# Softmax weights scaled where the output is written, the logarithm ahead of the dummy products, and a new instruction order, in a fused recurrence and soft-expert kernel

## The chip, the core and the metric

The kernel runs on one core of a Trainium2 chip. The metric is the device time of one execution in microseconds (us). The kernel before takes 120.81 us (median of three runs, 120.77 to 120.97). The core's engines run side by side, each with its own queue of instructions in program order: TensorE (PE; its weight loads are listed as PEld), VectorE (DVE), ScalarE (ACT), GpSimd (POOL) and SyncE (SP). An engine whose next instruction waits lets everything behind it wait as well.

## What is computed

There are two stages, one feeding the other.

```
# stage 1, for each of 4 batches x 8 heads, head width 48, 768 steps
cur   = (u * k_t) outer v_t
y_t   = r_t @ (state + cur)
state = w * state + k_t outer v_t
# stage 2, x is y as 3072 tokens x 384; 8 experts with 4 slots each
logits = x @ phi                       # 3072 x 32
d = softmax of logits over the tokens (each column)
slot_input = d.T @ x                   # 32 x 384
slot_out = relu(slot_input @ w1[e]) @ w2[e]      # for each expert e
c = softmax of logits over the slots (each row)
out = c @ slot_out                     # 3072 x 384, float32
```

The first softmax is called dispatch here, the second one combine.

## The kernel before, in words

**Stage 1.** The 768 steps are cut into six chunks `c` of 128 steps. In each chunk, k, r and v arrive by two transfers each (`iL0` to `iL35`, two for each k, r, v of a chunk, in that order). They are copied into a padded tile (`qk`, `qr`, `qv`, line 325), transposed by TensorE (`tk`, `tr`, `tv`, line 335) and evicted, with k and r multiplied by tables of powers of w (`ek`, `er`, line 345) and v plain (`ev`). Transposing back gives natural-layout copies (`bk`, `bv`, line 356; evictions `kn`, `vn`). For each of two batch pairs `bl` and two head halves, TensorE forms the scores (`A`, line 374), VectorE masks them (`M`, line 380, 24 of them), TensorE adds up the outputs (`Y`, lines 448 to 456), and `x` evicts them. The state products are `s` (lines 420 and 424), their evictions with decay `S` (line 432). The diagonal term with `u` needs `pr` (line 386, k times r, on VectorE or GpSimd), a small product `D` (line 396), its eviction `ds` and `dv` (line 403, v times `ds`), which `Y` adds.

**Stage 2** starts chunk by chunk. `X` transposes x, `xT` evicts it, `l` forms the logits and `lg` evicts them. The combine softmax of a chunk (function `slots`, lines 493 to 523) goes: `mx` row maxima (VectorE), `sb` subtraction (GpSimd or VectorE), `ex` exponential (ScalarE), `sr` row sums and reciprocals (VectorE), `cn` division with a fourfold copy (GpSimd or VectorE), `c` transposes (TensorE), `cT` eviction. The dispatch softmax runs over three groups of chunks: maxima `gm`, `gt`, `gr`, their exchange over partitions `gd`, `gb`, `gx`; `gs` subtraction, `ge` exponential, `dp` products, `acc` running sums, with the rescaling `gf`, `gg`, `am` between groups. The last group takes its maxima from logits formed a second time (`gl`, line 558).

**The last chain.** After the last `acc`, `rc` and `un` divide by the column sums; `h00` to `h11` (line 662) multiply by w1, `hs` applies the maximum with 0, `ht` transposes, `hT` evicts, `o00` to `o77` (line 689) multiply by w2 and `so` evicts the result. Then 24 products `p` (line 713), their evictions `oe` (line 716, ScalarE and VectorE in turn) and eight transfers write the output.

**Transfers.** GpSimd issues all loads of k, r, v (`iL`), w1 (`iW0` to `iW7`) and w2 (`iV0` to `iV6`, `iVa7` for seven eighths and `iVb7` for the last eighth of the last expert) on one queue. From the ninth on, each issue first waits until the load eight places before it has landed (line 271). w2 lands in the space that raw k, r, v held. Output transfers are issued by SyncE.

**The order** is written out by hand: `ORDER` lists all steps, and `Plan.emit` issues them as listed, so each engine's queue is that list cut down to its own steps. A token such as `qr0:1/D` means step `qr0`, buffer 1, engine D (DVE), A (ACT) or P (POOL). Dummy products (`fill`, line 220, 128x512 each) run at the start: three, then four ahead of the logarithm on line 259, which the tables of powers (`zt`, `ze`) need.

Of the kernel before, what the change touches and what calls it, by code (L numbers as in the profile page):

```python
# [12 lines left out]
ORDER = """
zb zc iL4 za zd:/A zt1 iL5 zt2 ze1 iL6 qk0:0/D ze2 iL7 zt3 tk00:0,0 iL8 zt0 ze3 iL9 tk01:1 ze0 iL10 qr0:1/D ek00
iL11 tr00:2,0 ek01 tr01:3 iL12 er00 qv0:0/A iL13 bk00:4,0 er01 bk01:5,1 iL14 pr0:0/D kn00:/A A000:0,0 tv00:0,0
qk1:1/A iL15 tv01:1 kn01:/D D0:2,0 M000 iL16 ev01:/A tk10:3,1 tk11:4 iL17 ev00:/D qr1:0/A A001:0,1 ek10 bv00:5,0
iL18 bv01:1,1 ek11 ds0:/A vn00:/A tr10:0,1 M001 iL19 tr11:3 qv1:1/A dv00:0/P s00:2,4,0 bk10:5,2 er10 A010:0,2
vn01:/A S100 bk11:0,0 iL20 qk2:0/D tv10:2,1 kn10:/A dv01:1/P er11 Y001:1 kn11:/A S101 s01:5,3,1 pr1:0/D ev10:/A
tv11:4 iL21 Y000:0,0 iL22 ev11:/A S110 D1:2,1 iL23 x000:/D ds1:/A x001:/A S111 iL24 bv10:5,2 qr2:1/A M010 bv11:4,3
iL25 X00:0,0 iL26 xT00:/D vn10:/A Y010:2,1 iL27 vn11:/D A011:0,1 x010:/A l00:1 dv10:0/P s10:3,0,2 M011 lg00:/A  # L20
tk20:5,0 tk21:4 S200 iL28 tr20:2,0 ek20 iL29 qv2:0/A Y011:1 S201 A100:0,0 iL30 s11:3,5,3 er20 dv11:1/P x011:/A M100
tv20:0,0 tv21:2 ev20:/A X01:1,1 iL31 S210 A101:0,2 xT01:/D iL32 ev21:/A Y100:3,2 S211 iL33 tr21:0 qk3:0/D x100:/A
l01:1 iL34 bv20:5,0 M101 qr3:1/A bv21:2,1 iL35 vn21:/D Y101:3 vn20:/A iW0 er21 A110:0,1 lg01:/A x101:/A ek21 iW1
X10:2,0 M110 pr2:0/P bk20:5,1 xT10:/A bk21:1,2 mx0 kn20:/A A111:0,0 kn21:/D Y110:0,3 M111 tk30:3,1 x110:/A tk31:4
s20:2,1,0 ek30 qv3:0/A ek31 A200:0,2 Y111:5 S300 iW2 D2:0,0 S301 sb0:0/P tv30:3,1 x111:/A M200 iW3 s21:4,2,1 ds2:/A
ex0 ev30:/A dv20:0/P X11:1,1 tr30:5,1 sr0 xT11:/A A201:0,1 S310 tv31:0 iW4 S311 tr31:3 er30 dv21:1/P ev31:/A l11:4
Y200:1,4 M201 bk30:2,0 lg11:/A qk4:0/A iW5 bv30:5,2 x200:/D A210:0,0 cn0:0/P bv31:0,3 er31 vn30:/A bk31:4,1 M210
iW6 Y201:1 vn31:/A pr3:0/P c0:3 qr4:1/A l10:5 kn30:/D A211:0,2 Y210:0,5 lg10:/D x201:/D s30:2,5,2 M211 kn31:/A
X20:1,1 x210:/A tk40:4,0 S400 cT0:/A tk41:0 xT20:/D A300:0,1 ek40 qv4:0/A Y211:2 iW7 M300 D3:3,1 l20:1 zu tr40:4,0
x211:/A S401 ds3:/A lg20:/A A301:0,0 iV0 tr41:2 er40 dv30:0/P tv40:3,0 M301 qk5:1/A X21:1,0 tv41:5 xT21:/D iV1  # L30
A310:0,2 ev40:/A er41 dv31:1/P l21:4 ek41 ev41:/A s31:1,2,3 M310 bk40:3,2 iV2 lg21:/A qr5:0/A bk41:0,0 pr4:0/P
bv40:5,0 S410 bv41:4,1 gm0 kn41:/A Y301:1 S411 kn40:/A gt0:0 A311:0,0 mx2 gr00 Y300:2,6 vn41:/A mx1 M311 tk50:3,1
vn40:/A tk51:0 Y310:4,7 ek50 x300:/A iV3 qv5:1/A A400:0,1 ek51 Y311:5 sb1:1/P M400 iV4 D4:2,0 x301:/A s40:3,0,0
sb2:0/P x311:/A X30:1,1 gd0 ex2 x310:/D iV5 ex1 gb0:5 A401:0,2 ds4:/A sr2 xT30:/A s41:4,2,1 dv40:0/P gx0 M401
X31:5,0 l30:1 xT31:/A gs0:/P S510 A410:0,0 lg30:/D Y401:4 S501 dv41:1/P M410 ge0 tr50:1,1 tr51:5 l31:0 er50
A411:0,2 iV6 lg31:/A tv50:0,1 er51 tv51:1 M411 ev50:/A pr5:0/P dp0:5 ev51:/A mx3 sr1 Y411:0 acc0 cn1:1/D Y400:5,0
S500 bv50:1,2 x401:/A sb3:1/D A500:0,2 x400:/D vn50:/A bv51:3,3 M500 c1:4 ex3 Y410:5,1 iVa7 vn51:/A D5:1,1 cn2:0/P
sr3 x410:/A A501:0,1 X40:3,1 x411:/D ds5:/A cT1:/A M501 iVb7 X41:5,0 xT40:/A cn3:1/P c2:1 l40:0 dv50:0/D xT41:/A
A510:0,0 dv51:1/P c3:4 cT2:/A M510 l41:3 Y501:5 cT3:/A Y500:1,2 lg41:/A lg40:/A S511 A511:0,1 x500:/A Y510:4,3 gm1
x501:/A mx4 gt1:3 M511 sb4:0/P X50:0,1 x510:/A ex4 xT50:/A sr4 Y511:2 gr10 cn4:0/P gl0:1 gd1 x511:/D gb1:5 l50:4  # L40
gr20 X51:0,0 gx1 lg50:/A c4:3 gf1:/D gs1:/P xT51:/D gg1 cT4:/A am1:/D gl1 ge1 l51:2 dp1:5 gr21 lg51:/A gd2 mx5
gb2:4 sb5:1/D acc1 ex5 gs2 gx2 sr5 ge2 gf2:/P dp2:0 gg2 cn5:1/D am2:/P c5:3 acc2 rc cT5:/D un1:/P un0 h10:1 h01:2
hs10:/D h00:5 hs01:/D h11:4 hs00:/D ht0:0 hs11:/D hT0:/D ht1:3 o00:1 hT1:/D o10 o20 o30 o40 o50 o60 o70 o77 so p0:2
p1:5 oe0 p2:4 oe1 p3:0 dm00 oe2 p4:3 oe3 p5:1 dm01 oe4 p6:2 oe5 p7:5 dm02 oe6 p8:4 oe7 p9:0 oe8 p10:3 dm04 oe9
p11:1 p12:2 oe10 p13:5 oe11 p14:4 oe12 p15:0 p16:3 oe13 oe14 p17:1 dm10 p18:2 oe15 oe16 p19:5 p20:4 oe18 oe17 p21:3
dm14 p22:0 oe20 oe19 p23:2 oe22 oe21 dm20 oe23 dm24
# [712 lines left out]
```

## Time and profile before

| what | value |
|---|---|
| median of the runs | 120.81 us |
| the profiled execution, whole | 120.92 us |
| its span, first to last instruction | 119.1 us |
| busy: PE, DVE, ACT, POOL | 79%, 82%, 61%, 60% of the span |
| moved by DMA | 24.67 MB, mean 207 GB/s |
| bytes on the loads' queue | 19.66 MB |

The span is the stretch that the profile covers; 1.8 us of the execution lie outside it. Times in rows are microseconds from the start of the span. In the page's strips the span is cut into 40 slices of 2.98 us; a digit is the share in tenths, 9 for 90% and more. A row of the timeline gives start, length, engine, line, operation, tiles written and read, and in brackets how long the engine was idle before it and what released it. Rows of one line are merged, x24 being 24 instructions; the lengths of neighbouring rows overlap a little, because an instruction starts before the one ahead has drained. A row of windows gives for a stretch its length, the busy time of each engine, the granted TensorE clock as a share, the busy share of the DMA engines and the rate.

### The profile page before, as it was taken

Reading aid. Unit: us, or ns where it says so; the run is one execution under the profiler, and the core shown is the slowest. Engines: PE = TensorE matmul, PEld = TensorE weight load, DVE = VectorE, ACT = ScalarE, POOL = GpSimd, SP = SyncE. Lnnn points to the kernel's source line nnn. Section 1 sums busy time; section 2 is a strip of 40 time slices with the busy share of each in tenths; the row PEclk is TensorE's granted clock in tenths of the full one; section 3 lists DMA queues with packets and bytes.
Section 4 is the critical chain, followed back from the end, with each engine's and each line's share of the span. In section 5 each row is a group of like instructions: output and inputs, shape, how many; then the busy total and the mean of one; then the engine's idle time right before and its main releaser. Section 6 shows DMA issues by size and latency. Waiting matters only on the chain.

```text
span 119.1 us, 3755 instructions
## 1 busy us (share of the span) xinstructions
...
## 2 busy tenths in 40 slices
...
PEclk9999999999999999999999999999985559999855
DMA  2999999999999999999999999999999991049994
GB/s 28 155 171 199 207 207 207 212 192 193 210 203 207 229 213 219 210 217 216 217 210 221 210 221 214 213 215 218 215 215 219 206 189 25 0 175 417 411 415 167
DMA packets 8992, 24.67 MB, mean 207 GB/s; under 512 B 1168, under 2 KB 6160, under 8 KB 8976
## 3 DMA queue, kind: packets, MB, share of 16 engines
q0 software_dynamic: 7632, 19.66, 86.1%
...
q8 instruction: 12, 0.20, 0.6%
q14 instruction: 4, 0.03, 0.1%
q10 hardware_dynamic: 24, 0.00, 0.0%
...
## 4 chain that ended last, share of the span: by engine, by line
PE 34%; DVE 29%; DMA 10%; issue 7%; POOL 7%; ACT 4%; DVEq 0%; POOLq 0%; ACTq 0%
DMA w_all<-in_moe_w_dram 10%; PE pG L335 8%; DVE AT L380 8%; PE pG L662 4%; POOL pr L386 3%; PE pG L713 3%; DVE S L432 3%; PE pG L356 3%; DVE cn L510 2%; PE pG L689 2%; PE pA L374 2%; DVE rT L345 2%; DVE dv L403 2%; PE pA L222 2%; ACT rp L199 2%
## 5 line engine op out<-in xcount | busy, mean ns | idle before, releaser
L380 DVE TENSOR_TENSOR AT<-pA,mask 128x1024 bf16<-128x1024 f32 x24 | 29.1, 1214 | 0.2
L335 PE MATMUL pG<-ident,rp 128*128 128x128 bf16 x288 | 21.0, 230 | 3.0 <-DVE rp L201 3.0
L199 ACT COPY rp<-raw 128x1536 bf16<-128x1536 bf16 x14 | 20.8, 1486 | 3.5 <-PE pG L335 1.8
L335 PEld LDWEIGHTS <-rp 128*128 128x128 bf16 x288 | 18.2, 103 | 4.8 <-DVE rp L201 3.9
L403 POOL TENSOR_TENSOR dv<-vn,ds 128x768 bf16<-128x768 bf16 x11 | 16.3, 1480 | 3.2 <-ACT vn L199 2.0
L386 POOL TENSOR_TENSOR pr<-kT,rT 128x2048 bf16<-128x2048 bf16 x4 | 16.3, 4067 | 1.5 <-DVE rT L345 0.9
L199 ACT COPY w_all<-pG 128x384 f32<-128x384 f32 x12 | 4.9, 499 | 12.3 <-PE pG L713 12.3
L199 ACT COPY vT<-pG 128x1024 bf16<-128x1024 bf16 x11 | 10.8, 1025 | 1.8 <-PE pG L335 1.8
L432 DVE TENSOR_TENSOR S<-pG,W 128x384 bf16<-128x384 f32 x20 | 10.8, 546 | 0.0
L374 PE MATMUL pA<-rT,kT 64*128 64x128 bf16 x192 | 9.6, 218 | 0.4 <-DVE AT L380 0.3
L454 PE MATMUL pG<-vn,AT 128*128 128x48 bf16 x192 | 8.7, 183 | 1.2 <-DVE AT L380 1.2
L199 ACT CAST x<-pG 128x384 bf16<-128x384 f32 x17 | 8.2, 498 | 2.1 <-PE pG L456 2.1
L199 ACT COPY vn<-pG 128x768 bf16<-128x768 bf16 x10 | 7.9, 815 | 1.0 <-PE pG L356 1.0
L356 PE MATMUL pG<-ident,vT 128*128 128x128 bf16 x96 | 6.7, 219 | 1.9 <-DVE S L432 1.9
L211 POOL DMA_DIRECT2D raw<-in_k_dram x12 | 6.6, 564 | 2.6 <-DMA raw<-in_v_dram 1.8
L211 POOL DMA_DIRECT2D raw<-in_v_dram x12 | 6.8, 579 | 2.2 <-DMA raw<-in_r_dram 2.2
L345 DVE TENSOR_TENSOR kT<-pG,Tk 128x1024 bf16<-128x1024 bf16 x12 | 7.8, 681 | 0.3 <-ACT Tk L299 0.3
L454 PEld LDWEIGHTS <-AT 128*128 128x128 bf16 x192 | 7.0, 96 | 1.7 <-DVE AT L380 1.7
L345 DVE TENSOR_TENSOR rT<-pG,Tr 128x1024 bf16<-128x1024 bf16 x12 | 8.0, 680 | 0.0
L456 PE MATMUL pG<-dv,ident 128*128 128x384 bf16 x24 | 7.7, 323 | 0.3 <-DVE dv L403 0.3
L374 PEld LDWEIGHTS <-kT 64*128 64x128 bf16 x192 | 5.8, 94 | 2.8 <-issue 1.2
L211 POOL DMA_DIRECT2D raw<-in_r_dram x12 | 6.6, 562 | 1.0 <-DMA raw<-in_k_dram 0.9
(123 smaller groups left out, 213.9 us busy)
## 6 DMA issues: line engine op xcount, KB each, us to landing
w_all<-in_moe_w_dram POOLq DMA_DIRECT2D x8, 768.0 KB, 15.0
raw<-in_moe_w_dram POOLq DMA_DIRECT2D x7, 768.0 KB, 23.8
out_dram<-w_all SPq DMA_DIRECT2D x5, 768.0 KB, 4.8
raw<-in_k_dram POOLq DMA_DIRECT2D x12, 192.0 KB, 6.7
raw<-in_r_dram POOLq DMA_DIRECT2D x12, 192.0 KB, 6.5
raw<-in_v_dram POOLq DMA_DIRECT2D x12, 192.0 KB, 6.7
...
out_dram<-w_all SPq DMA_DIRECT2D x2, 192.0 KB, 2.0
```

What stands on the lines that cost most here:

```text
L199: O(act.copy(dst, src))
L211: O(pool.dma_start(out=raw_t(x)[:, bb * JJ * D:(bb + 1) * JJ * D], in_=src[c, bb]))
L335: O(pe.transpose(o[:, :, j, :], rp_r[W[rp]][:, jh * JH + j].rearrange("p b d -> p (b d)"), ident[:]))
L345: O(dve.tensor_mul(dst, src, (Tk, Tr)[which][:, None, jh].to_broadcast(BC)))
L356: O(pe.transpose(bank_b(kb)[:, h * C:(h + 1) * C], src[:, bl, h].rearrange("p a x -> p (a x)"), ident[:]))
L374: O(pe.matmul(pA[:, bb, h4 * C:(h4 + 1) * C], kt[s, bl, h].rearrange("p a x -> p (a x)"), rt[s, bl, h].rearrange("p a x -> p (a x)"), star ...
L380: O(dve.tensor_mul(AT_r[W[f"AT{key}"]][:], pA[:].rearrange("p bb (h t) -> p bb h t", t=C), mask[:, None, None, :].to_broadcast([128, 2, H ...
L386: O(op(e).tensor_mul(pr_r[W[f"pr{c}"]][:], kT_r[W[f"kT{c}"]][:].rearrange("p a h j x -> p a h (j x)"), rT_r[W[f"rT{c}"]][:].rearrange("p a ...
L403: O(op(e).tensor_mul(dv_r[W[f"dv{c}{bl}"]][:], vn_r[W[f"vn{c}{bl}"]][:], ds_r[W[f"ds{c}"]][:, bl, :, :, None].to_broadcast([128, H, 2, D])))
L432: O(dve.tensor_mul(S_r[W[new]][:, s], bank(kb[hf])[:, 0:HD].rearrange("p (h b d) -> p h b d", b=2, d=D), W128[:, s, :, None].to_broadcast( ...
L454: O(pe.matmul(o[:, z:z + D], AT_r[W[at]][:, bb, h4, :], vn[:, hf * H2 + h4, bb, :], start=(c == 0 and h4 == 0 and bb == 0), stop=False, sk ...
L456: O(pe.matmul(o[:, 0:HD], ident[:], dv_r[W[f"dv{c}{bl}"]][:, hf * H2:(hf + 1) * H2] .rearrange("p h b d -> p (h b d)"), start=False, stop= ...
```

## The change

1. **Combine softmax.** `sb`, `sr` and `cn` are gone. `mx` writes the negated maximum; `ex` is four ScalarE instructions for a chunk (one for each batch) that read the logits four times over, take the maximum as bias and write the unnormalised weights in bfloat16 straight to `cn`'s tile. The row sums come from TensorE: `rs`, 24 products with a column of 32 ones, and `rr`, one reciprocal. The evictions `oe` multiply by it.
2. **Start.** The logarithm stands ahead of the four dummy products. Two small memsets (line 248 and 249 of the new file) fill the column of ones.
3. **Dummy products** `F0` to `F24`, one 128x512 product each, stand between the steps of the last chain.
4. **Order.** The whole list is new. `dv` is on GpSimd always.

```diff
@@ slots
-        P.add(f"sb{c}", "POOL|DVE", lambda e: O(op(e).tensor_sub(
-            ee_r[W[f"ee{c}"]][:], lg, mx[:, c, :, None].to_broadcast([128, B, ES]))), deps=[f"mx{c}"],
-            take=[(f"ee{c}", "ee")])
         def ex(e):
-            t = ee_r[W[f"ee{c}"]]
-            O(act.activation(out=t[:], in_=t[:], func=AF.Exp))
+            for b in range(B):
+                O(act.activation(out=cn_r[W[f"cn{c}"]][:, b], in_=lg_all[:, c * B + b:c * B + b + 1, :]
+                                 .to_broadcast([128, 4, ES]), func=AF.Exp, bias=mx[:, c, b:b + 1]))
-            O(dve.tensor_reduce(out=sm[:, c], in_=ee_r[W[f"ee{c}"]][:], axis=AX.X, op=ALU.add))
-            O(dve.reciprocal(sm[:, c], sm[:, c]))
-        P.add(f"cn{c}", "POOL|DVE", lambda e: O(op(e).tensor_mul(
...
@@ new steps
+    def sums(e):
+        for i in range(3 * JH):
+            g, j = divmod(i, JH)
+            O(pe.matmul(bank("rsb")[:, i:i + 1], cT[:, j, g * 128:(g + 1) * 128], one_s[:], start=(i == 0), stop=True,
+                        skip_group_check=True))
+    P.add("rr", "DVE", lambda e: O(dve.reciprocal(rcs[:], bank("rsb")[:, 0:3 * JH])), deps=["rs"], use=["rsb"])
@@ eviction of the output
-                    e, obuf[:, i * Dm:(i + 1) * Dm], bank(kb)[:, 0:Dm]), deps=[f"p{i}"], use=[kb]))
+                    if e == "ACT":
+                        O(act.mul(dst, src, rcs[:, i:i + 1]))
+                    else:
+                        O(dve.tensor_scalar(out=dst, in0=src, scalar1=rcs[:, i:i + 1], scalar2=None, op0=ALU.mult))
@@ start
+    O(act.activation(out=lnw[:], in_=pA[:, 1, 0:H], func=AF.Ln))
     fill(4)
-    O(act.activation(out=lnw[:], in_=pA[:, 1, 0:H], func=AF.Ln))
@@ dummy products
+FILL = [("gt1", 3), ("gl0", 2), ("X51", 3), ("gl1", 3), ("dp1", 3), ("gb2", 4), ("dp2", 4), ("acc2", 3)]
+    for after, count in FILL:
+        for x in range(count):
+            P.add(f"F{n}", "PE", lambda e: fill(1), deps=[after, f"F{n - 1}" if n else None])
```

The new order, cut down to the queues that the prediction speaks of (a minus is before, a plus is after):

```diff
 VectorE, start
- zb za zt1 zt2 qk0 zt3 zt0 qr0 ek00 ek01 er00 er01
+ zt1 zt0 zt2 zt3 qk0 za zb qr0 ek00 ek01 er00 er01
 GpSimd
- iL19 dv00 iL20 dv01 iL21 iL22 iL23 iL24 iL25 iL26 iL27 dv10 iL28 ... iL35 iW0 iW1 pr2 iW2 sb0 iW3 dv20 iW4 dv21
+ iL19 dv00 iL20 dv01 iL21 iL22 pr1 iL23 iL24 iL25 iL26 iL27 iL28 dv10 iL29 dv11 iL30 ... iL35 dv20 iW0 iW1 iW2 iW3 dv21
- iW7 zu iV0 dv30 iV1 dv31 iV2 pr4 iV3
+ iW7 iV0 pr3 iV1 zu dv30 iV2 dv31 iV3 pr4 iV4 dv40 iV5 dv41 gs0 pr5 iV6 iVa7 dv50 iVb7 dv51
 VectorE, end
- M511 sr4 gr10 gd1 x511 gr20 gx1 gf1 xT51 am1 gr21 gd2 mx5 sb5 acc1 gs2 gx2 sr5 cn5 acc2 rc cT5 un0 hs10 hs01 hs00 hs11 hT0 hT1 so
+ M511 gm1 mx4 x511 gr10 gr20 gd1 xT51 gx1 gs1 gr21 gd2 mx5 acc1 gs2 gx2 gf2 cT5 acc2 rc un0 hs00 hs11 hs10 hT1 rr hs01 hT0 so
 ScalarE, end
- ex4 xT50 lg50 gg1 cT4 ge1 lg51 ex5 ge2 gg2
+ xT50 ex4 lg50 cT4 gg1 ge1 lg51 ex5 ge2 gg2
 TensorE, end
- gl0 gb1 l50 X51 c4 gl1 l51 dp1 gb2 dp2 c5 h10 h01 h00 h11 ht0 ht1 o00
+ gt1 F0 gl0 l50 X51 F1 c4 gb1 F2 gl1 l51 F3 F4 F5 F6 dp1 gb2 F7 c5 F8 F9 F10 dp2 F11 ... F17 h00 h11 h10 F18 ... F22 ht1 F23 rs F24 h01 ht0 o00
```

Across the whole list, VectorE loses six `sr`, two `cn`, two `sb`, one `dv`, one `am`, two `x` and one `xT`, and takes over from ScalarE or GpSimd two padded copies `q`, one `kn`, one `vn`, one `ev`, three `ds`, two `lg`, one `cT` and `gs1`. The numbers of masks, state evictions, `ek`, `er` and `pr` (two on VectorE, four on GpSimd) stay. `pr1` goes from VectorE to GpSimd, `pr2` the other way.

More of the change, by code (lines that the diff above doesn't have):

```diff
@@ L16 @@
[L16 to L20, printed above, removed]
@@ L31 @@
[L31 to L35, printed above, removed]
@@ L41 @@
[L41 to L45, printed above, removed]
```

79 lines of the change are left out of this document (48 added, 31 removed).

## The prediction

> **What bounds the kernel now.** I read the page's strips first, then a table of windows that cuts the span where the stages change, then the timeline at the seams.
>
> ```profile
> span 119.1 us, 3755 instructions
> ...
> PEclk9999999999999999999999999999985559999855
> DMA  2999999999999999999999999999999991049994
> ```
>
> ```profile
> 9.94:63.41 53.47, 51.03 (x954) 44.16 (x953) 52.20 (x82) 46.85 (x63) 46.37 (x54) 1.00 1.10 210
> 63.41:87.27 23.86, 19.78 (x386) 16.30 (x385) 23.38 (x40) 14.17 (x30) 15.26 (x14) 1.00 1.04 215
> 87.27:94.20 6.93, 4.83 (x81) 3.58 (x81) 5.43 (x21) 2.40 (x8) 2.04 (x4) 0.59 1.04 215
> 94.20:100.58 6.38, 6.13 (x64) 2.67 (x65) 3.37 (x6) 0.00 (x0) 0.00 (x0) 0.65 0.68 133
> 100.58:103.44 2.86, 2.78 (x65) 1.71 (x65) 0.69 (x1) 0.00 (x0) 0.00 (x0) 1.00 0.03 6
> 103.44:119.10 15.66, 4.89 (x24) 2.21 (x23) 6.22 (x13) 4.94 (x12) 0.00 (x0) 0.79 0.75 301
> ```
>
> Busy columns are PE, PEld, DVE, ACT, POOL, then granted clock, DMA share, GB/s. Up to 63.41 VectorE (52.20 of 53.47) and TensorE (51.03) are both full. From there to 87.27, where the last x is evicted, VectorE alone is full and TensorE is idle for 23.86 - 19.78 = 4.1 us. Then a chain of small steps runs at a falling clock, the w1 products at about half clock, the w2 products, and 15.66 us of output, which is a matter of transfers (301 GB/s on average) and which I hold fixed. Independently of all this, the DMA strip is at 9 from 3 us to about 98 us: the loads are a second bound. Where do they end?
>
> ```profile
> 76.04 0.59 POOL L217 DMA_DIRECT2D raw<-in_moe_w_dram  x1
> ```
> ```profile
> raw<-in_moe_w_dram POOLq DMA_DIRECT2D x1, 96.0 KB, 24.1
> ```
>
> The last eighth of w2 is issued at 76.04 and lands 24.1 us later, at 100.15. o77 needs it, and `so` needs o77. Now `so` starts at 103.44, so **whatever the engines gain, 3.2 us is the most that can be won** unless the loads end earlier, and every delay of the loads eats into that.
>
> **Start.** Terms 1 to 4 give when the w2 products can be done, term 5 when the loads let them.
>
> ```profile
> 5.89 0.18 ACT L259 ACTIVATE lnw<-pA 128x8 f32<-128x8 f32 x1 [3.25 <-PE pA L222]
> ...
> 9.44 0.51 POOL L211 DMA_DIRECT2D raw<-in_v_dram  x1 [0.49 <-DMA raw<-in_r_dram]
> ...
> 9.94 0.55 DVE L201 COPY rp<-raw 128x1536 bf16<-128x1536 bf16 x1
> ```
>
> (1) The logarithm loses its wait on the dummy products (3.25 us idle). What is late next is data: qr0, the copy at 9.94, needs the second r transfer, whose landing releases GpSimd at 9.44. In the new VectorE queue qr0 stands ahead of ek00, so VectorE stands there till 9.44. Gain 9.94 - 9.44 = 0.5 us, not 3. The two memsets and zd, za, zb fit in that wait.
>
> **The body.**
>
> ```profile
> L510 DVE TENSOR_TENSOR cn<-ee,sm 128x512 bf16<-128x512 f32 x2 | 3.6, 1815 | 0.0
> ...
> L403 DVE TENSOR_TENSOR dv<-vn,ds 128x768 bf16<-128x768 bf16 x1 | 2.0, 1974 | 0.0
> L201 DVE COPY kn<-pG 128x768 bf16<-128x768 bf16 x3 | 1.7, 551 | 0.0
> ...
> L507 DVE TENSOR_REDUCE sm<-ee 128x4 f32<-128x128 f32 x6 | 1.6, 274 | 0.0
> ...
> L497 DVE TENSOR_TENSOR ee<-lg_all,mx 128x128 f32<-128x128 f32 x2 | 1.1, 563 | 0.1
> ...
> L508 DVE RECIPROCAL sm<-sm 128x4 f32<-128x4 f32 x6 | 1.1, 178 | 0.2
> ```
>
> (2) VectorE loses 3.6 (cn) + 2.0 (dv) + 1.6 + 1.1 (sums, reciprocals) + 1.1 (subtractions) = 9.4 us, and 3 x 0.55 for two x and an xT, priced like the copy of L201: 11.0. It takes over five such copies (two q, kn, vn, ev: 2.8, a little more for the larger ev) and seven small steps that I put at 0.25 each (ds, lg, cT, gs1, between the 0.178 and 0.563 of the rows): about 4.6 in all. Net 6.4 us. About 1.3 of it (the fifth chunk's sr, cn and subtraction) lie behind the last x, so 5.1 lie ahead. The order puts 1 us of that ahead of 63.41, where TensorE has only 53.47 - 51.03 = 2.4 us idle to give, and some 4.1 behind it, as much as TensorE's idle time there. I take all of it and give back 0.3 for new waits: 4.8. With term 1 the last x is evicted at 87.27 - 5.3 = **82.0**. Bounds: 81.0 if the inflated cn also leaves no wait behind it, 85.2 if TensorE takes the lead and two thirds are lost.
>
> ScalarE takes 24 exponentials. Their form isn't in the trace; the nearest row is a 128x128 one, the far end that of 128x384.
>
> ```profile
> L503 ACT ACTIVATE ee<-ee 128x128 f32<-128x128 f32 x6 | 1.8, 337 | 3.2 <-DVE ee L497 3.1 <-POOL ee L497 0.2
> ...
> L586 ACT ACTIVATE dx<-dd 128x384 bf16<-128x384 f32 x1 | 0.5, 523 | 0.0
> ...
> L586 ACT ACTIVATE dx<-dd 128x128 bf16<-128x128 f32 x1 | 0.3, 309 | 0.4 <-DVE run L578 0.4
> ```
>
> 24 x 0.309 = 7.4 us (12.6 at the far end) against 6 x 0.34 before; five copies leave ScalarE, which is idle 23.86 - 14.17 = 9.7 us in the second stretch. Hidden, except ex5 in the last chain.
>
> (3) **The last chain**, counted from the last x. Before: 6.93 to the first w1 product, 6.38 to o00, 2.78 of w2, end at 103.4.
>
> ```profile
> 85.10:88.50 3.40, 2.45 (x30) 1.00 1.03 211
> 95.30:98.70 3.40, 3.40 (x36) 0.50 0.91 178
> ```
> ```profile
> 94.20 4.98 PE L662 MATMUL pG<-w_all,uns 128*32 128x512 bf16 x48 [0.78 <-POOL uns L643]
> ```
>
> The clock fell to half after a stretch with TensorE 2.45 of 3.40 busy and rose after one with 3.40 of 3.40. 48 w1 products, four side by side, are 12 passes of 0.415 us at half clock; 0.21 at full clock. A dummy product of the same width is one pass: 0.21.
>
> The Trainium skill, page "TensorE: Matmul & The Clock Gate", Part 1 (the HAM clock gate), says the clock halves after an idle window of about 3.4 us and rises after a busy one. The rise agrees with the row 95.30:98.70. The fall does not: no window here was idle. By the page the dummy products have nothing to prevent; by the row they do, and may also be too few.
>
> Count with the clock up. The first steps (X51, xT51, gl1) take 2.2 us as before: F0 to F2 and c4 take back what the clock gives. F3 to F6 (0.85), dp1 (0.85) and gb2 come next: 4.4. gs2 is at 4.8, but ge2 stands behind ex5's four instructions on ScalarE: 5.2. F8 to F10 (0.65) and dp2 (0.5): 6.5. acc2, rc, un: 7.5, but F11 to F17 (1.5) hold TensorE till 8.0. That is 1.1 later than before. Three w1 products at 0.63: 9.9. F18 to F22: 11.0. ht1, F23 and `rs`: 12.2. For `rs`, 24 narrow products, the nearest row is this:
>
> ```profile
> 63.41 0.54 PE L396 MATMUL pG<-ucol,pr 128*128 128x2 bf16 x16
> ```
>
> 24/16 x 0.54 = 0.8 (0 to 1.3, as the pieces overlap or run at half clock). F24 and the last w1 product: 13.1; its eviction, ht0, hT0: 15.4. Before it was 13.3. So the dummy products and the late h01 give back more than the clock gains: o00 at 97.4, w2 done 2.8 later at **100.2**.
>
> (4) The new evictions `oe` read a scalar for each row.
>
> ```profile
> L199 ACT COPY w_all<-pG x12: 478/485/552, 104.4 to 108.9; 128x384 f32<-128x384 f32 x12
> L201 DVE COPY w_all<-pG x12: 546/547/558, 104.6 to 109.7; 128x384 f32<-128x384 f32 x12
> ```
>
> They are done at 109.7 now, long before the transfers end at 119.1. Cost 0; bounds -0.5 and +0.5, about one eviction, which is how much earlier or later the first transfer could leave.
>
> (5) **The loads.** Here is the catch.
>
> ```profile
> 21.61 1.73 DVE L386 TENSOR_TENSOR pr<-kT,rT 128x2048 bf16<-128x2048 bf16 x1
> ```
> ```profile
> L386 POOL TENSOR_TENSOR pr<-kT,rT 128x2048 bf16<-128x2048 bf16 x4 | 16.3, 4067 | 1.5 <-DVE rT L345 0.9
> ```
> ```profile
> 22.73 1.05 POOL L211 DMA_DIRECT2D raw<-in_v_dram  x2
> ```
> ```profile
> raw<-in_v_dram POOLq DMA_DIRECT2D x1, 192.0 KB, 5.3
> ```
> ```profile
> raw<-in_k_dram POOLq DMA_DIRECT2D x1, 192.0 KB, 3.7
> ```
>
> pr1 moves from VectorE (21.61) into GpSimd's queue between iL22 and iL23, and takes 4.07 us there. It can start when ek11 is done, at about 21.9 by the running sum of term 2, and iL22 ends about then. So iL23 leaves at 26.1 instead of about 23.2 (the second of the two at 22.73). The 5.3 us row is that load, landing at 28.5; the 3.7 row is the very first load, on an empty queue, the least that a load takes. So iL23 can't land ahead of 26.1 + 3.7 = 29.8: the queue runs dry and **the whole stream is 1.3 us late**, since nothing in the DMA strip's nines gives it back. Vb7 lands at 101.45 instead of 100.15, o77 follows at about 101.7. The Trainium skill, page "DMA: Bandwidth & Descriptors", section "Anatomy of one DMA", puts the fixed part of such a transfer at about 2 us; by 2.0 plus its rate term the delay would be near 0; the measured 3.7 decides.
>
> **Sum.** The later of 100.2 (engines) and 101.7 (loads), against 103.4: 1.7 us off 120.92, so **119.2 us**. The profiled execution lies 0.1 above the median of 120.81, inside the runs' own spread.
>
> **Rivals.**
>
> *The loads are not delayed* (pr1 starts sooner, or the queue holds out): Vb7 at 100.15, `so` at 100.6, engines level with it: 120.92 - 2.9 = 118.0. For it: the stream in 28 to 34 us has small hitches of its own that may vanish. Against: the 4.07 us row. Chance 0.15.
>
> *The engines bind.* TensorE is as full as VectorE up to 63.41, and GpSimd waits for landings before it gets to pr4, dv40, dv41. Last x at 84.5, w2 done at 102.7: 120.2. Chance 0.17.
>
> *The clock falls anyway.* Dummy products then run at 0.42 and so fill TensorE, which raised the clock after one window in the row above; one or two windows at half speed cost 1.7 to 3.4: w2 done at 101.9 to 103.6, near 120.5. Chance 0.08.
>
> *Slower: w1 is issued behind dv20.*
>
> ```profile
> 33.94 0.62 POOL L214 DMA_DIRECT2D w_all<-in_moe_w_dram  x1
> ...
> 41.78 1.49 POOL L403 TENSOR_TENSOR dv<-vn,ds 128x768 bf16<-128x768 bf16 x1
> ```
> ```profile
> w_all<-in_moe_w_dram POOLq DMA_DIRECT2D x1, 768.0 KB, 10.2
> ```
>
> iW0, now at 33.94 and landing 10.2 later at 44.1, moves behind dv20, which ran at 41.78. A w1 load is four times an iL (0.95 us of transfer each at 207 GB/s), so alone it takes the 3.7 of an iL and some 2.7 more: 6.4, an estimate. By the running sum dv20 has its inputs at 36.9 and iW0 leaves at 38.4: 44.8, within the delay already counted. But each us more goes one to one into Vb7. If dv20 stays at 41.78, iW0 leaves at 43.3 and lands at 49.7, the stream is 5.6 late, o77 is at 106 and the time 123.5. The change turns into a loss once dv20 starts after 39.2. Half way, 40.5, gives 122.2. Chance 0.2.
>
> **How the numbers follow.** Forecast 0.40; the rivals 0.15, 0.17, 0.08, 0.20. About 0.2% (0.24 us) is what a measurement of this kernel can tell from no change. Faster: 0.40 + 0.15 + 0.12 + 0.03 = 0.70; same 0.07; slower 0.23. Range: down to the undelayed loads with 0.3 to spare, up to a dv20 about 0.8 us past the turning point: 117.7 to 121.7.
>
> **What would show it.** Right: iL23's issue near 26 behind a 4 us pr on GpSimd and Vb7's landing near 101.5; the last x near 82; granted clock 1.00 from there on; w1 products near 0.21 us a pass; TensorE waiting for a landing ahead of the last w2 products. Wrong: a DMA strip without a dip near 27 us, w2 products that never wait, a clock row under 1.00 between 85 and 98, or a GpSimd dv ahead of the first w1 load at 40 or later.

## The result, and the profile after

The changed kernel takes **125.09 us** (median of 4 runs, 123.53 to 126.33) against 120.79 us (4 runs, 120.70 to 120.97) on the same chip: ratio 1.031, 95% interval 1.021 to 1.041. Forecast were 119.2 us and a range of 117.7 to 121.7, so the sign is wrong as well as the size. The profiled execution took 125.33 us. All ratios in this document leave out slow executions, in which the clock was lower or the time over 1.5% above the fastest of the same kernel; the profiles of e10 and e12 are of such executions, so their `so` includes a lower clock in the last chain and is listed only.

The page's strips of the changed kernel, and its instruction queue:

```profile
span 123.5 us, 3853 instructions
...
PEclk9999999779999999999999999999999999999655
DMA  2999999947999999999999999999999995089990
GB/s 28 163 195 205 207 208 207 205 79 116 172 163 159 159 220 219 215 216 211 219 214 213 216 217 214 211 219 214 215 213 219 214 210 105 2 312 400 416 394 12
...
q8 instruction: 13, 0.21, 0.6%
```

The forecast's dip is there, but it is no notch: the ninth and tenth slice (24.7 to 30.9 us) move 79 and 116 GB/s, and the four after them still 159 to 172. The clock, which had dropped to half in the last chain of before, stays at 1.00 from 63.41 up to `so`. The table of windows of the changed kernel, cut at the same seams (busy PE, PEld, DVE, ACT, POOL, then granted clock, DMA share, GB/s):

```profile
9.94:63.41 53.47, 48.82 (x891) 42.67 (x889) 49.74 (x74) 43.73 (x62) 41.80 (x48) 0.97 1.03 188
63.41:85.71 22.30, 21.04 (x436) 17.45 (x433) 20.50 (x37) 16.13 (x34) 16.32 (x12) 1.00 1.04 215
85.71:93.98 8.27, 8.11 (x100) 5.03 (x99) 5.12 (x19) 4.06 (x14) 1.45 (x4) 1.00 1.04 215
93.98:101.74 7.76, 6.02 (x96) 3.28 (x96) 4.37 (x7) 0.00 (x0) 0.00 (x0) 1.00 1.04 214
101.74:106.25 4.51, 3.28 (x64) 1.71 (x65) 0.00 (x1) 0.00 (x0) 0.00 (x0) 1.00 0.43 79
106.25:123.50 17.25, 5.47 (x24) 2.21 (x23) 6.95 (x13) 5.77 (x12) 0.00 (x0) 0.76 0.69 275
```

The seams are the last x (85.71; before 87.27, forecast 82.0), the first w1 product (93.98), o00 (101.74), `so` (106.25; before 103.44) and the end. All four stretches behind the last x are longer than before. The first two, 8.27 and 7.76 against 6.93 and 6.38, were forecast so in kind. The w2 products, 4.51 against 2.86, and the output, 17.25 against 15.66, were not. TensorE's timeline tells what the w2 products wait for:

```profile
101.74 2.46 PE L692 MATMUL pG<-raw,rT 128*32 128x384 bf16 x56 [0.78 <-DVE rT L203]
105.39 0.82 PE L692 MATMUL pG<-raw,rT 128*32 128x384 bf16 x8 [1.19 <-DMA raw<-in_moe_w_dram]
```

The loads end last, as forecast, but the last part of w2 is issued at 81.21 and lands 24.6 us later, at 105.8 instead of 101.45 (by the DMA view):

```profile
raw<-in_moe_w_dram POOLq DMA_DIRECT2D x1, 96.0 KB, 24.6
```

GpSimd's timeline shows where the loads were held:

```profile
23.16 4.06 POOL L390 TENSOR_TENSOR pr<-kT,rT 128x2048 bf16<-128x2048 bf16 x1 [1.17 <-DVE kT L349]
27.16 0.56 POOL L213 DMA_DIRECT2D raw<-in_v_dram  x1
...
29.73 0.60 POOL L213 DMA_DIRECT2D raw<-in_v_dram  x1
31.95 1.48 POOL L407 TENSOR_TENSOR dv<-vn,ds 128x768 bf16<-128x768 bf16 x1 [1.63 <-ACT ds L201]
33.37 0.59 POOL L213 DMA_DIRECT2D raw<-in_v_dram  x1
33.97 1.49 POOL L407 TENSOR_TENSOR dv<-vn,ds 128x768 bf16<-128x768 bf16 x1
35.39 1.08 POOL L213 DMA_DIRECT2D raw<-in_k_dram  x2
...
38.77 1.48 POOL L407 TENSOR_TENSOR dv<-vn,ds 128x768 bf16<-128x768 bf16 x1 [0.22 <-ACT cn L504]
40.19 2.23 POOL L216 DMA_DIRECT2D w_all<-in_moe_w_dram  x4
```

Before, the same stretch looked like this:

```profile
26.77 1.47 POOL L403 TENSOR_TENSOR dv<-vn,ds 128x768 bf16<-128x768 bf16 x1 [0.92 <-ACT vn L199]
28.19 1.08 POOL L211 DMA_DIRECT2D raw<-in_v_dram  x2
29.23 0.55 POOL L211 DMA_DIRECT2D raw<-in_k_dram  x1
```

Behind pr1 stands iL23, issued at 27.16 (before 23.23). Then dv10 waits 1.63 us for ds1, the eviction of D1, and iL29 stands behind it (33.37; before 28.73, the second of the two at 28.19); iL30 stands behind dv11 (35.39; before 29.23); iW0 behind dv20 (40.19; before 33.94).

The late stream reaches TensorE by a second path as well. iV0 must wait until the load eight places before it, W0, has landed (49.7; before 44.1), and pr3 stands behind iV0 (GpSimd's timeline, then TensorE's):

```profile
50.03 0.53 POOL L219 DMA_DIRECT2D raw<-in_moe_w_dram  x1 [3.10 <-DMA w_all<-in_moe_w_dram]
50.58 4.08 POOL L390 TENSOR_TENSOR pr<-kT,rT 128x2048 bf16<-128x2048 bf16 x1
```
```profile
54.71 0.55 PE L400 MATMUL pG<-ucol,pr 128*128 128x2 bf16 x16 [1.84 <-POOL pr L390]
```

In the same way pr4 stands behind iV3, which waits for W3, and TensorE waits another 0.68 us for it.

In the table, landings and steps of one profiled execution of each kernel, in us. "Out" is from `so` to the end of the span, "code" the packets in the instruction queue.

| kernel | L23 | L30 | W0 | Vb7 | last x | so | out | code | time | ratio, interval |
|---|---|---|---|---|---|---|---|---|---|---|
| before | 28.5 | 35.7 | 44.1 | 100.2 | 87.3 | 103.4 | 15.7 | 12 | 120.8 | |
| changed | 31.0 | 40.3 | 49.7 | 105.8 | 85.7 | 106.2 | 17.2 | 13 | 125.1 | 1.031 (1.021-1.041) |
| e1 | 28.6 | 38.8 | 48.8 | 104.9 | 84.9 | 105.3 | 17.3 | 13 | 124.7 | 1.031 (1.024-1.037) |
| e2 | 28.0 | 37.1 | 46.7 | 102.7 | 82.3 | 103.1 | 17.5 | 13 | 122.9 | 1.015 (1.008-1.022) |
| e2, no dummies | 28.4 | 38.5 | 47.7 | 103.8 | 83.4 | 104.2 | 16.1 | 12 | 122.1 | 1.010 (1.003-1.018) |
| e3 | 28.8 | 35.6 | 44.0 | 100.1 | 84.6 | 101.7 | 16.0 | 12 | 119.8 | 0.990 (0.986-0.993) |
| e5 | 28.8 | 39.0 | 48.6 | 104.7 | 92.1 | 111.0 | 17.2 | 13 | 130.0 | 1.079 (1.075-1.084) |
| e6 | 30.9 | 39.0 | 48.6 | 105.0 | 89.0 | 106.6 | 16.0 | 12 | 124.3 | 1.031 (1.026-1.035) |
| e7 | 28.3 | 35.7 | 44.3 | 100.6 | 84.6 | 101.1 | 16.1 | 12 | 119.0 | 0.991 (0.984-0.997) |
| e8 | 28.7 | 35.5 | 44.2 | 100.3 | 84.6 | 100.7 | 16.1 | 12 | 118.4 | 0.983 (0.980-0.987) |
| e9 | 28.4 | 35.4 | 44.2 | 100.3 | 84.5 | 101.2 | 17.4 | 13 | 120.5 | 0.998 (0.995-1.000) |
| e10 | 28.5 | 36.4 | 46.4 | 102.4 | 84.5 | 104.7 | 15.8 | 12 | 121.7 | 0.994 (0.990-0.999) |
| e11 | 28.4 | 39.5 | 51.0 | 107.1 | 92.4 | 107.5 | 16.0 | 12 | 125.3 | 1.038 (1.032-1.044) |
| e12 | 28.4 | 35.9 | 44.3 | 100.1 | 85.7 | 105.3 | 15.8 | 12 | 122.3 | 1.001 (0.995-1.006) |
| e13 | 31.8 | 40.0 | 48.4 | 104.5 | 90.8 | 108.1 | 15.8 | 12 | 125.3 | 1.033 (1.028-1.039) |

### The profile page after: what moved, and what is told of

Its sections match the earlier page's. It is cut to its first block, busy times and chain, and to the rows that moved or that the text cites. A ratio compares the mean times of both kernels' runs of the same rounds, so it can differ in the third digit from the quotient of the medians.

```text
span 123.5 us, 3853 instructions
## 1 busy us (share of the span) xinstructions
PE 99.3 (80%) x1630; PEld 75.9 (61%) x1633; DVE 94.1 (76%) x179; ACT 74.5 (60%) x129; POOL 66.7 (54%) x81
## 4 chain that ended last, share of the span: by engine, by line
DMA 35%; PE 21%; POOL 18%; DVE 8%; ACT 5%; issue 5%; DVEq 0%; POOLq 0%
DMA raw<-in_moe_w_dram 23%; POOL pr L390 10%; DMA w_all<-in_moe_w_dram 8%; PE pG L339 7%; DVE w_all L724 5%; PE pG L360 4%; DMA raw<-in_r_dram 4%; POOL dv L407 4%; POOL raw L219 2%; PE pA L378 2%; PE pG L428 1%; POOL raw L213 1%; ACT rp L201 1%; PE pG L458 1%; DVE rT L349 1%
## 5 line engine op out<-in xcount | busy, mean ns | idle before, releaser
L407 POOL TENSOR_TENSOR dv<-vn,ds 128x768 bf16<-128x768 bf16 x12 | 18.0, 1500 | 5.1 <-ACT ds L201 2.1
L201 ACT COPY rp<-raw 128x1536 bf16<-128x1536 bf16 x12 | 17.7, 1479 | 5.0 <-DMA raw<-in_v_dram 3.7
L722 ACT ACTIVATE w_all<-pG,rcs 128x384 f32<-128x384 f32 x12 | 5.8, 613 | 15.6 <-PE pG L716 15.6
L201 ACT CAST x<-pG 128x384 bf16<-128x384 f32 x19 | 9.0, 487 | 4.0 <-PE pG L460 3.8
L224 PE MATMUL pA<-ones 128*128 128x512 bf16 x29 | 9.4, 438 | 1.6 <-DVE ones L233 1.5
L504 ACT ACTIVATE cn<-lg_all,mx 128x128 bf16<-128x128 f32 x24 | 7.7, 403 | 3.1 <-DVE mx L499 3.1
L201 ACT COPY xT<-pG 128x768 bf16<-128x768 bf16 x8 | 6.4, 803 | 3.7 <-PE pG L478 3.7
L428 PE MATMUL pG<-vn,kn 128*128 128x96 bf16 x80 | 6.5, 207 | 2.1 <-DVE rT L349 2.1
L201 ACT COPY vn<-pG 128x768 bf16<-128x768 bf16 x9 | 7.1, 810 | 1.8 <-PE pG L360 1.7
L219 POOL DMA_DIRECT2D raw<-in_moe_w_dram x9 | 5.2, 581 | 5.0 <-DMA w_all<-in_moe_w_dram 4.6
```

The source lines that it names most:

```text
L201: O(act.copy(dst, src))
L224: O(pe.matmul(pA[:, 0, :], ones[:, 0:128], ones[:], start=True, stop=True))
L407: O(op(e).tensor_mul(dv_r[W[f"dv{c}{bl}"]][:], vn_r[W[f"vn{c}{bl}"]][:], ds_r[W[f"ds{c}"]][:, bl, :, :, None].to_broadcast([128, H, 2, D])))
```

## The experiments

**Theory:** what is lost is lost in GpSimd's queue, where the new order puts products that are late ahead of loads that are due; the parts of the change other than the order gain. **Rivals:** the dummy products cost the time; the new order is late on the other engines too; the new softmax is slower. One more path lies between the theory and the second rival: a GpSimd product that comes late makes TensorE wait at once, whenever w2 lands. No run sets it apart by itself, but the traces of e5, e6, e11 and e13 show it.

### The loads ahead of pr1 (e1)

```diff
- iL22 pr1 iL23 iL24 iL25 iL26
+ iL22 iL23 iL24 iL25 pr1 iL26
```

> The changed kernel with one move in GpSimd's queue: iL23, iL24 and iL25 ahead of pr1 instead of behind it. They cost GpSimd nothing, since it stands idle before pr1 until 23.16. Loads theory (the whole loss is the load stream running dry behind GpSimd's work, and every hole adds): the hole at iL23 (2.5 us of the 5.65 by which the last w2 load is late) closes, the last load lands near 103.3 and the time falls by 2 to 2.6 us from 125.1, to 122.5 to 123. Engine theory (the new order and the dummy products make the engines' own chain longer, the loads only come on top): w2 products can't be done before 104.5, so the gain stops at 1.7 us, 123.4 or more. If the hole only moves (a later load is then the late one), nothing changes: 125.

124.67 us, no gain that can be told. L23 landed on time (28.6) and at L30 the stream was 3.1 us late again, behind dv10 and dv11. Mending one hole alone moves the loss to the next.

### All loads ahead (e2), and without the dummy products

```diff
- iL22 pr1 iL23..iL28 dv10 iL29 dv11 iL30 .. iL35 dv20 iW0 iW1
+ iL22 iL23 iL24 iL25 pr1 iL26..iL29 dv10 iL30 iL31 dv11 iL32 .. iL35 iW0 iW1 dv20
- iV0 pr3 ... iV3 pr4
+ pr3 iV0 ... pr4 iV3
```

> The changed kernel with all loads put ahead of the GpSimd work that held them: iL23 to iL25 ahead of pr1, iL29 ahead of dv10, iL30 and iL31 ahead of dv11, iW0 and iW1 ahead of dv20; and the other way round, pr3 ahead of iV0 and pr4 ahead of iV3, so that they don't stand behind a wait for a landing (49.7 and 61.0 in the changed kernel). Loads theory: the last load lands at 100.2 to 100.8 as before the change, pr3 and pr4 start 3 to 4 us earlier and the last x comes near 83; the time is 119.5 to 121. Engine theory: the loads land at 100.5 too, but the w2 products are done only at 103 to 104.5 and the time stays at 122 to 123.5.

122.87 us: some 2 us won by the order of GpSimd's queue alone. The run moves the loads and pr3 and pr4 together, so it doesn't say what each is worth; TensorE's waits for pr3 and pr4 are gone. The loads are still 2.6 us late, and the last x, evicted from 81.79 on in e2's timeline of VectorE, is at 82.35:

```profile
81.79 0.56 DVE L203 CAST x<-pG 128x384 bf16<-128x384 f32 x1
```

> The kernel with all loads first, without the 25 dummy products of the last chain. If the dummy products hold the clock up and stand in nobody's way, leaving them out lets the clock fall to half near 88 as before the change, the w1 products take 0.42 us a pass instead of 0.21, and the end of the w2 products comes 1 to 2.5 us later. If they cost as much as they bring (they stand ahead of dp1, dp2, the first w1 product and ht1 in TensorE's queue), the time is the same within 0.5 us, and where the loads bind it is the same in any case.

122.13 us, which the intervals don't tell from e2. The clock fell (0.68 from 90 to 97 us). `so` came 1.0 us later, but not by the clock: the last x and the landing of Vb7 are 1.1 and 1.0 later too, and from the last x to `so` it is 20.7 us here and 20.8 in e2. The loads bind, as the last part of the expectation has it. The output stage is 1.4 us shorter (16.1 against 17.5). So the dummy products hold the clock up, and cost something where no dummy product stands.

### The order of before with the new softmax (e3)

The list of before, with sb, sr and cn dropped, `rs` behind the last group of w1 products, the logarithm ahead, no dummy products.

> The order of before the change, with the new combine softmax (exponentials in four instructions, sums by TensorE, scaling at the output), the logarithm ahead of the dummy products, and no dummy products in the last chain: the parts of the change without its order. Loads theory: GpSimd's queue only loses work, the load stream has no new hole, the last load lands at 99.5 to 100.5, the last x comes 2 to 5 us ahead of 87.3, and the time is 118.3 to 120. Rival (the parts themselves cost something: 7.7 us of exponentials on ScalarE, 0.61 us instead of 0.50 for a scaled eviction, 1.6 us more between so and the end): 121 to 123 with the loads on time.

119.76 us, 1.0% less than before, clear of the noise (ratio 0.986 to 0.993). The softmax is not what costs the time: with the queue of before the loads are on time (100.1) and the last x is 2.6 us earlier than before. The windows of e3 around the last chain show what is left there:

```profile
88.50:91.78 3.28, 1.46 (x25) 1.12 (x23) 1.80 (x7) 1.49 (x6) 1.00 (x3) 0.60 1.05 216
91.78:96.61 4.83, 4.83 (x51) 1.78 (x52) 2.08 (x4) 0.00 (x0) 0.00 (x0) 0.56 1.03 212
```

The w1 products, from 91.78 on, run 4.83 us at half clock.

### GpSimd's queue of before in the new order (e5)

```diff
- pr1 on GpSimd, pr2 on VectorE; iL26 iL27 iL28 dv10 iL29 dv11 iL30 ..
+ pr1 on VectorE, pr2 on GpSimd; iL26 iL27 dv10 iL28 iL29 iL30 dv11 iL31 .. iL35 iW0 iW1 pr2 iW2 iW3 dv20 ..
```

> The changed kernel with its own order on TensorE, VectorE and ScalarE, but the queue of GpSimd in the order of before: pr1 on VectorE, pr2 on GpSimd, each load at its old place among the products; the dummy products stay. If the loads held back in that queue are what cost the time: the last w2 part lands at 100.1 to 100.8 (after 105.84), last x at 81.7 to 82.8, the last output product ends at 101.0 to 101.6, and with 13 packets of code and 17.3 us of output stage the time is 120.3 to 121.1 us. If the order on the other engines is late by itself: last x at 84 or later, w1 product after 92.5, the last output product after 103, 122 to 123.5 us, with the loads landed by 101.

130.03 us, which neither theory had. GpSimd's timeline of e5:

```profile
31.91 1.47 POOL L407 TENSOR_TENSOR dv<-vn,ds 128x768 bf16<-128x768 bf16 x1 [7.05 <-ACT ds L201]
33.34 1.11 POOL L213 DMA_DIRECT2D raw<-in_v_dram  x2
```

dv10 waited 7.05 us for ds1, with iL28 behind it. pr1 wasn't the cause; it was done on VectorE by 24.1. The diagonal D1 simply stands late in TensorE's new queue: it starts at 30.97 in e5, and as late in the changed kernel, where it doesn't wait for anything:

```profile
31.02 0.54 PE L400 MATMUL pG<-ucol,pr 128*128 128x2 bf16 x16
```

This hold isn't what sets e5 apart, though: from L30 on its loads land ahead of those of the changed kernel (W0 48.6 against 49.7, Vb7 104.7 against 105.8), and o00 starts at 108.2, when w2 has long landed. What does is pr2. This run puts it on GpSimd behind iW1, and TensorE waits for it:

```profile
44.27 0.58 PE L400 MATMUL pG<-ucol,pr 128*128 128x2 bf16 x16 [7.54 <-POOL pr L390]
```

So e5 is no test of the loads. That a queue suits one order of the other engines says nothing about another. It leaves open whether the new order is late by itself.

### pr1 on GpSimd in the old order (e6, e11)

```diff
- s01 pr1:VectorE ev10 .. iL22 iL23
+ s01 ev10 .. iL22 pr1:GpSimd iL23          (e6)
+ s01 ev10 .. iL22 iL23 .. iL27 pr1:GpSimd iL28   (e11, with nine dummy products)
```

> The kernel with the order of before and the new softmax (119.76 us), with one product moved: pr1 from VectorE to GpSimd's queue, right behind load 22, as in the changed kernel. If a hole in the load stream is never made good: load 23 lands 2.0 to 2.8 us later (28.5 to about 31), dv10 and the loads behind it follow, the last w2 part lands at 102.5 to 103.5, and the time is 121.8 to 123 us. If the stream takes a hole of 4 us up again (as the prediction had it, 1.3 us): the last w2 part at 101.4 or earlier and 119.8 to 121.0 us.

> The kernel with nine dummy products (118.41 us), pr1 on GpSimd as in the run that cost 4.5 us, but behind load 27 in place of load 22. If it is the loads held behind pr1 that cost, and pr1's own lateness only through them: loads 23 to 27 land as in the kernel with nine dummies (28.7 to 32.6), pr1 runs at about 25.3 to 29.4, load 28 is issued 0.5 to 1.5 us later and lands at 34 to 35, the last w2 part at 100.3 to 101.5, 118.4 to 119.6 us. If pr1 on GpSimd costs by itself (first diagonal late, dv10, dv11 and the loads behind them late): the last w2 part at 103 or later, 121 us or more.

124.26 and 125.30 us, against 119.76 and 118.41. e6 seemed to price the hole, but TensorE's timelines (e6, then e11) say that it doesn't do so alone:

```profile
27.29 0.58 PE L400 MATMUL pG<-ucol,pr 128*128 128x2 bf16 x16 [4.64 <-POOL pr L390]
```
```profile
30.09 0.59 PE L400 MATMUL pG<-ucol,pr 128*128 128x2 bf16 x16 [7.24 <-POOL pr L390]
```

In the old order D1 stands early in TensorE's queue, and everything behind it waits for pr1. So e11 fell with loads 23 to 27 on time: the rival that pr1's own lateness costs holds there. In e6 the w2 products do not wait for w2, in e11 by some 0.1 us. In the changed kernel D1 doesn't wait; both runs left the price of the hole open there.

### Dummy products behind the end, and tiny ones ahead of it (e7, e9)

```diff
+ FILL = [("p23", 18)]                                   (e7, on e3)
+ o70, then 20 products of one column, then o77          (e9, on e8)
```

> The kernel with the order of before and the new softmax (119.76 us), and 18 dummy products behind the last output product, for which nothing waits. If a 13th packet of code during the output transfers is what lengthens the output stage: 13 packets in the instruction queue, one DMA engine's output packets trailing the others by 1 to 1.6 us, output stage 17.2 to 17.6 us in place of 16.05, 120.8 to 121.3 us. If the longer output stage of the kernels with dummies has another cause (the scaled evictions, the state of the clock): 12 or 13 packets and 119.4 to 120.1 us, no trailing engine.

> The kernel with nine dummy products (118.41 us), and 20 dummy products of one column (31 ns each by the row of the sums) while TensorE waits for the last w2 part, so that TensorE's program is as long as the changed kernel's. If the length of the program brings a 13th packet of code into the output transfers and that lengthens the stage: 13 packets before the last output packet, one DMA engine trailing by 1 to 1.6 us, the output stage 17.2 to 17.6 us in place of 16.1, 119.5 to 120.1 us. If the longer stage has another cause: 118.2 to 118.7 us, no trailing engine.

e7 was no test: its 13th packet came after the last output packet, so its 119.03 us tell nothing of the cause. e9 is one. The 13th packet came, `so` is only 0.5 us later than in e8, and the output stage went from 16.1 to 17.4; 120.52 us against 118.41, by the ratios to before some 1.8 us more. The windows at the end of the transfers, e8 and then e9:

```profile
114.00:115.00 1.00, 0.00 (x0) 0.00 (x0) 0.00 (x0) 0.00 (x0) 0.00 (x0) 0.50 0.76 307
115.00:116.00 1.00, 0.00 (x0) 0.00 (x0) 0.00 (x0) 0.00 (x0) 0.00 (x0) 0.50 0.00 0
```
```profile
115.00:116.00 1.00, 0.00 (x0) 0.00 (x0) 0.00 (x0) 0.00 (x0) 0.00 (x0) 0.50 0.31 123
116.00:117.00 1.00, 0.00 (x0) 0.00 (x0) 0.00 (x0) 0.00 (x0) 0.00 (x0) 0.50 0.06 25
117.00:118.00 1.00, 0.00 (x0) 0.00 (x0) 0.00 (x0) 0.00 (x0) 0.00 (x0) 0.50 0.00 0
```

A DMA share of 0.06 is the work of one engine of 16: it ends about a us after the others. The changed kernel ends the same way:

```profile
120.00:121.00 1.00, 0.00 (x0) 0.00 (x0) 0.00 (x0) 0.00 (x0) 0.00 (x0) 0.50 0.31 123
121.00:122.00 1.00, 0.00 (x0) 0.00 (x0) 0.00 (x0) 0.00 (x0) 0.00 (x0) 0.50 0.04 18
```

In the table all five kernels with 13 packets have an output stage of 17.2 to 17.5, all ten with 12 one of 15.7 to 16.1.

### Nine dummy products (e8), the fastest kernel

```diff
+ FILL = [("gt1", 2), ("gb2", 4), ("c5", 3)]             (on e3)
```

> The kernel with the order of before and the new softmax (119.76 us; clock at half from 89.0 to 95.5), with 9 dummy products in TensorE's idle places of the last chain: 2 ahead of gl0, 4 behind gb2, 3 behind c5. If the clock falls for want of work there: granted clock 1.00 to 96, w1 product ends at 94 to 95, the output product then waits for the last w2 part at 100.1 and ends at 100.9 to 101.1, 12 packets of code, 118.9 to 119.4 us: little, since the loads bound it. If the dummies only delay the chain or the clock falls anyway: 119.7 to 120.3. If 9 already bring the 13th packet: 120.3 to 120.9.

**118.41 us**, ratio 0.983 (0.980 to 0.987), a little under the 118.9 to 119.4 expected. The clock stays up, and in TensorE's timeline the w1 products take 2.77 us in place of 4.83:

```profile
91.76 2.77 PE L665 MATMUL pG<-w_all,uns 128*32 128x512 bf16 x48
...
96.76 2.46 PE L692 MATMUL pG<-raw,rT 128*32 128x384 bf16 x56
99.86 0.82 PE L692 MATMUL pG<-raw,rT 128*32 128x384 bf16 x8 [0.65 <-DMA raw<-in_moe_w_dram]
```

Of the 2.1 us won there `so` keeps 1.0: the last product now waits for w2. This is the bound that the prediction named.

### The loads free in the new order (e10, e12), and pr1's hole alone (e13)

```diff
+ pr1:VectorE, iL21 .. iL31 dv10 iL32 iL33 dv11 iL34 iL35 iW0 .. iW3 dv20     (e10, nine dummy products)
+ pr1:VectorE, iL21 .. iL35 iW0 dv10 iW1 dv11 iW2 iW3 dv20                    (e12, twelve dummy products)
+ iL21 iL22 pr1:GpSimd iL23 .. iL35 iW0 dv10 iW1 dv11 iW2 iW3 dv20            (e13, else as e12)
```

> The changed kernel's order with pr1 on VectorE, every load moved ahead of the products on GpSimd that held it back (loads 28 to 31 ahead of dv10, w1 parts 0 to 3 ahead of dv20, w2 parts 0 and 1 behind pr3), and 9 dummy products in place of 25. If the hold in GpSimd's queue and the 13th packet are the whole loss: w1 part 0 lands at 44 to 44.6, the last w2 part at 100.1 to 100.8, last x at 82 to 84, the output product ends at 100.7 to 101.6, 12 packets, 118.2 to 119.3 us. If the order on the other engines costs time by itself: the loads land by 100.8 and the output product ends after 102, 120 us or more.

> The changed kernel's order with pr1 on VectorE, loads 21 to 35 and w1 part 0 ahead of dv10, w1 parts 2 and 3 ahead of dv20, w2 parts 0 and 1 behind pr3, and 12 dummy products (2 ahead of gl0, 3 behind gb2, 3 behind dp2, 4 behind the third group of w1 products). If the hold in GpSimd's queue is what made the changed kernel slow: w1 part 0 lands at 44 to 45, the last w2 part at 100.1 to 101, the output product ends at 100.7 to 101.6, 12 packets of code, 118.2 to 119.3 us. If the order of the other engines is late by itself: loads as above, but the output product ends after 102.5, 120 us or more.

> e12 with one product moved: pr1 on GpSimd between loads 22 and 23, as in the changed kernel, and nothing else. The prediction's price for that hole was 1.3 us at the end of the stream: last w2 part 1.3 us behind e12's. By the changed kernel's trace load 23 landed 2.5 us late and nothing is made up while the stream is full: 2.3 to 3.0 us behind e12's, and the time 2.0 to 3.0 us above it. If the delay of the chunk behind pr1 comes on top: 4 us or more.

e10 didn't free the loads: dv10 waits 4.04 us for ds1 with iL32 behind it, and Vb7 lands at 102.4. So neither of its expectations is tested (ratio 0.994).

e13 differs from e12 by pr1 alone, and D1 doesn't wait for it. GpSimd's timeline of e13, and iL23's row in the DMA view of e12 and of e13:

```profile
24.21 4.07 POOL L390 TENSOR_TENSOR pr<-kT,rT 128x2048 bf16<-128x2048 bf16 x1 [1.17 <-DVE kT L349]
28.23 0.56 POOL L213 DMA_DIRECT2D raw<-in_v_dram  x1
```
```profile
raw<-in_v_dram POOLq DMA_DIRECT2D x1, 192.0 KB, 5.3
```
```profile
raw<-in_v_dram POOLq DMA_DIRECT2D x1, 192.0 KB, 3.6
```

iL23 leaves at 28.23 in place of 23.11, 5.12 late: pr1's 4.07 and the wait for its operand. The queue had 5.3 - 3.6 = 1.7 in hand; L23 lands 3.4 later (31.8 against 28.4) and Vb7 4.4 later. In the stream the hole is not made good. The time goes from a ratio of 1.001 to 1.033, some 3.9 us, near the third of the three expectations, but not because w2 comes late: Vb7 has landed at 104.5 when o00 starts at 105.25. dv10 stands behind the same issues as the loads and starts at 39.26, in e12 at 35.15, and TensorE waits for it (TensorE's timeline of e13):

```profile
40.80 0.48 PE L460 MATMUL pG<-dv,ident 128*128 128x384 bf16 x1 [6.77 <-POOL dv L407]
```

In e12 this wait is 1.31. The 5.5 us between them are about the 5.1 by which the last x is later. So e13 shows what the hole costs the stream; what late loads alone would cost in time, with no product of GpSimd behind them, no run shows.

e12 has the loads on time and 12 packets and is level with before, not at 118.2 to 119.3: the second expectation. Its last x is at 85.7; in e2, with dv10 ahead of loads that in e12 stand ahead of dv10, and with pr1 on GpSimd, it is at 82.3. What each of the two makes of the 3.4 us was not tested. The new last chain is also longer than the old: from the last x to o00 it takes 16.0 us in the changed kernel with 25 dummy products (85.7 to 101.74), 14.4 in e13 with twelve (90.84 to 105.25), and 12.1 in e8 in the old order with nine (84.6 to 96.76), with the clock up in all three. No queue that was tried gave the new order both the loads and the early last x. An estimate of both together from these rows is 82.3 + 16.0 + 2.9 = 101.2 for `so` with 25 dummy products, behind e8's 100.7. With e13's chain it is 99.6; then the landing of w2 at 100.2 would bind as it does in e8, and the two orders would be level. So whether the new order loses by itself, with a better queue and fewer dummy products, stays open.

## Why the prediction was wrong, point by point

**(5), the loads, is the step that failed: its mechanism was right, its size was 1.3 us and measured 5.65.** "iL23 leaves at 26.1" took pr1 to start at 21.9, straight behind iL22. It started at 23.16, behind a wait of 1.17 us for kT, and iL23 left at 27.16. It landed 3.8 us later, about the least that the prediction had (3.7), 2.5 us late. The other 3.2 the prediction did not look for. It priced the one thing that was moved ahead of the loads and stopped. dv10 and dv11 stand among the same loads as before, but the new order brings their operand late (D1 at 31.02; before 23.39). L30, issued at 35.39 behind both, landed 2.4 us behind L29: the queue had run dry again, and that made the stream 1.5 later. Two more steps, 1.2 at L26 and 0.9 at L33, came with loads that had been issued 6.3 and 7.3 us ahead of landing, so no hold in the queue explains them; their cause stays open. At L30 the stream was 4.6 late, at W0 5.6, at Vb7 5.65. e1 shows that the second hole costs 3.1 by L30 without the first, e13 that pr1 by itself makes 4.4 in this order.

The Trainium skill, "DMA: Bandwidth & Descriptors", section "Anatomy of one DMA", puts the fixed part of a transfer at about 2 us. iL23 met an empty queue and took 3.8 us from issue to landing, 3.6 in e13, so the measured value decides here as well.

**The output stage, held fixed at 15.66, is the second miss**: 17.25. The dummy products lengthen TensorE's program, which brings the 13th packet of code among the output transfers. That makes about 1.3 of the 1.6 us (e9 against e8: 17.4 - 16.1).

Both add up: `so` at 106.25 against 103.44 - 1.7 = 101.7 forecast is 4.5, the output 1.6, together 6.1, and 119.2 + 6.1 = 125.3.

**(1) Start.** Right in kind, and the wait that was forecast stands in VectorE's timeline of the changed kernel, at the copy that was at 9.94:

```profile
8.77 0.56 DVE L203 COPY rp<-raw 128x1536 bf16<-128x1536 bf16 x1 [1.34 <-DMA raw<-in_r_dram]
```

It gives 1.2 us, not 0.5. It comes with the new order of VectorE's first steps: in e3, with the logarithm ahead and the old order, this copy was at 9.84. How much it gives hangs on the second r transfer: in the other kernels with this start the copy is at 8.40 (e5) to 9.41 (e2 without dummy products).

**(2) Body, the third miss.** The last x is at 85.7, not 82.0. The subtraction of VectorE's work was right: from 9.94 to the last x it is busy for 49.74 + 20.50 = 70.2 us, before for 52.20 + 23.38 = 75.6. What was not counted are the waits for landings in GpSimd's queue ahead of pr3 and pr4, by which the late stream reaches TensorE (1.84 and 0.68 us). In e2, with these waits gone and the loads less late, the last x is at 82.35, near the forecast; no run takes these waits away alone. This miss alone would have turned the sign: without any wait for w2 the w2 products of the changed kernel end at about 101.74 + 2.8 = 104.5 (2.8 is what they took before), not at 100.2, and before had `so` at 103.44.

**(3) Last chain.** Right. From the last x to o00 16.0 us (15.4 forecast), clock 1.00, `rs` 0.74 us (0.8): as forecast, 25 dummy products and the late h01 cost more than the clock gives. e13, with twelve of them, takes 14.4; the old chain of e8, with nine, 12.1.

**(4) Evictions.** Right within its bounds. By the list of instruction groups ScalarE's scaled eviction takes 613 ns against 485 for the plain one, and the exponentials 7.7 us against 7.4 forecast:

```profile
L504 ACT ACTIVATE cn<-lg_all,mx 128x128 bf16<-128x128 f32 x24 | 7.7, 403 | 3.1 <-DVE mx L499 3.1
...
L722 ACT ACTIVATE w_all<-pG,rcs 128x384 f32<-128x384 f32 x12 | 5.8, 613 | 15.6 <-PE pG L716 15.6
```

With 12 packets the output stage of the new softmax is 15.7 to 16.1, so the evictions cost 0 to 0.4.

**Rivals.** The slower one named the right queue and nearly the right time (122.2 to 123.5 for loads held behind dv20), but not the right place: dv20 started at 38.77, ahead of the turning point of 39.2, and the load ahead of W0 (L35, at 46.1) was 5.7 late already. It looked at one of three products on the same path whose operands the new order could bring late; dv10 and dv11 got no chance at all. The clock did not fall ahead of `so`. *The engines bind* was nearer than its 0.17 says: it named the waits for landings ahead of GpSimd's products, and its last x (84.5) and its end of the w2 products (102.7) were nearer the measured 85.7 and 104.5 than the forecast's. It did not decide the end, because w2 landed at 105.8, after the first 56 w2 products were done at 104.2.
